# An mLSTM layer and its expert MLP on one core: weight loads on a second queue, low weight parts on GpSimd, one run of k times v, and a new order

## The chip, the cores and the metric

The kernel runs on one core of a Trainium2 chip. A core has five engines that work side by side, each through its own queue in program order: TensorE (PE, matmuls), VectorE (DVE), ScalarE (ACT), GpSimd (POOL) and SyncE (SP), which here only issues DMAs. An instruction that has to wait for another engine holds everything behind it on its own queue. The metric is the device time of one execution in microseconds (us). The time before is 543.33 us, the median of 543.33, 537.8 and 544.72.

## The reference

Four sequences with eight heads of width 40 run through a gated recurrence of 768 steps; its output, 3072 tokens by 320, runs through an MLP with 2048 hidden channels:

```
m_new = max(f[t] + m, i[t])
C = exp(f[t]+m-m_new) * C + exp(i[t]-m_new) * v[t] k[t]^T
n = exp(f[t]+m-m_new) * n + exp(i[t]-m_new) * k[t]
y[t] = sigmoid(o[t]) * (C q[t]) / max(|n q[t]|, 1)
h = y @ w_in;  g = h * erf(softplus(h));  out = g @ w_out
```

The two weights, w_in (320 x 2048) and w_out (2048 x 320), come as float64, eight bytes a number.

## The kernel before

The recurrence is done in 6 chunks of 128 time steps. An attention step s is one chunk c of one sequence b (s = 4c + b, 24 in all). It takes exponentials of gate differences (`pe`, `ex`), masks them on GpSimd (`sel`), multiplies them with q times k (`S`, `w`), sums over v (`ph`), and carries a state per sequence (`pk`, `sk`, `sa`): k times v, weighted (`vg`), is added to the state after each chunk but the last. `den`, `yg`, `y` finish the columns of y, `tr` turns them on TensorE, and `xh`, `xl` take them out of PSUM as a high and a low part. From chunk 1 on q and k are themselves split into high and low parts (`khi`, `klo`, `qhi`, `qlo`) and stacked by DMAs from `parts` to `stk`.

Two attention steps give 256 tokens. For these the MLP runs in 4 groups of 512 hidden channels, so there are 48 groups. A group has `up` (32 matmuls, h from x and w_in, line 818), a chain of activations that alternates between ScalarE and VectorE (`hb`, `a`, `a2`, `sq`, `b`, `ah`, `ab`, `w`, `wh`, `gh`, `gl`), and `dn` (24 matmuls with w_out, lines 887, 888, 890). Every matmul operand is kept as a high part and a low part; `gh` (line 868) and `gl` (line 873) are those of the MLP's middle. The first `dn` of a group needs `gh`, the last ones `gl`.

The weights are decoded on the chip, in 26 pieces: 16 of w_out (128 x 320, named `('o', n)`) and 10 of w_in (128 x 512, `('i', part, k)` and the tails `('t', i)`, the last 64 rows of two parts). A piece is scaled on ScalarE (`val`, line 707), gets its low mantissa bits by three VectorE operations (`bits`, lines 712, 713, 715), is rounded to the high part on ScalarE (`hi`, line 720), and gives the low part through TensorE: `dif` multiplies the value with the identity and subtracts the high part in PSUM (lines 725, 726), from where ScalarE copies it (`lo`, line 730). The raw bytes are loaded by SP: w_out into tiles called `parts`, two of them, three pieces each; w_in into the ten buffers that the MLP uses later as `hb`, `n0`, `n1`, `gh`, `gl`. All loads go over SP's one queue.

The order of all instructions on all engines is written out by hand: each part has a number in a table (`ATT`, `MLP`, `DEC`, `LOAD` and others), which is added to the start of its unit, and the program emits the parts sorted by that sum. So a queue's content follows from the tables, and a part waits on its engine where the data aren't there yet.

Of the kernel before, what the change touches and what calls it, by code (L numbers as in the profile page):

```python
# [99 lines left out]
ATT_NEXT = {'load': -108.5865,  # L100
    'loadv': -65.7264,
    'khi': -43.9486,
    'qhi': -36.8481,
    'klo': 33.0974,
    'qlo': 4.1048,
    'stk0': -62.7653,
    'stk1': 33.0459,
    'rows': -112.0,
    'pe0': -92.4353,
    'pe1': -82.6231,  # L110
    'ex0': -85.3469,
    'ex1': -74.7973,
    'sel0': -83.8594,
    'sel1': -59.1013,
    'S0': -64.4044,
    'S1': -29.3249,
    'vg0': -46.0099,
    'vg1': -19.402,
    'w0': -39.4592,
    'w1': -14.1493,  # L120
    'th': -41.0893,
    'pq': -109.6295,
    'qa': -38.5364,
    'ph0': -10.0541,
    'ph1': -6.3375,
    'ph2': 5.1946,
    'ph3': 6.4602,
    'pk0': -35.9301,
    'pk1': -7.3506,
    'sa0': 27.0234,  # L130
    'sa1': -6.4202,
    'sk0': -34.6458,
    'sk1': -0.3263,
    'den': 17.2106,
    'yg': 28.411,
    'y': 30.5578,
    'tr': 34.3008,
    'xh': 35.0968,
    'xl': 36.9102}
ATT = {'load': -38.0873,  # L140
    'loadv': -22.0289,
    'khi': -26.4131,
    'qhi': -24.304,
    'klo': -21.0673,
    'qlo': -20.9744,
    'stk0': -13.01,
    'stk1': -20.7116,
    'rows': -35.0,
    'pe0': -16.191,
    'pe1': -27.6979,  # L150
    'ex0': -14.5235,
    'ex1': -17.8549,
    'sel0': -13.8199,
    'sel1': -15.9236,
    'S0': -5.8456,
    'S1': -11.6692,
    'vg0': -8.7917,
    'vg1': -11.6286,
    'w0': -5.765,
    'w1': -10.6719,  # L160
    'th': -5.5334,
    'pq': -27.7455,
    'qa': -20.3849,
    'ph0': 1.4564,
    'ph1': 1.6614,
    'ph2': 2.8445,
    'ph3': 3.6732,
    'pk0': 6.9497,
    'pk1': -1.5624,
    'sa0': 7.8642,  # L170
    'sa1': 7.8309,
    'sk0': 10.4729,
    'sk1': 17.4327,
    'den': 7.2966,
    'yg': 10.4519,
    'y': 11.8501,
    'tr': 12.5049,
    'xh': 15.9467,
    'xl': 18.6409}
# [803 lines left out]
```

## Time and profile before

| | |
|---|---|
| Time, median of three | 543.33 us (537.8 to 544.72) |
| The profiled execution | 542.79 us, span 541.1 us |
| Mean granted TensorE clock | 0.987 |
| TensorE busy | 521.8 us (96%) |
| VectorE, ScalarE busy | 435.9 us (81%), 448.2 us (83%) |
| GpSimd busy | 92.4 us (17%) |
| Moved by DMA | 58.85 MB, of which 33.40 MB read from HBM |
| DMA queues of the program | one, q1 |

The profiled execution took 1.69 us more than its span from the first to the last instruction. Matmuls are pipelined: the length of one in a row (282 ns for a 128 x 256) is longer than the distance to the next (about 0.12 us), so costs on TensorE are read from the starts of successive rows. Shares of busy time are a mean over stages; the program has a start of about 48 us in which weights and first inputs arrive, a stretch up to about 150 us in which decoding, attention and MLP overlap, a regular part up to about 520 us, and an end.

### The profile page before, as it was taken

Reading aid. Unit: us, or ns where it says so; the run is one execution under the profiler, and the core shown is the slowest. Engines: PE = TensorE matmul, PEld = TensorE weight load, DVE = VectorE, ACT = ScalarE, POOL = GpSimd, SP = SyncE. Lnnn points to the kernel's source line nnn. Section 1 sums busy time; section 2 is a strip of 40 time slices with the busy share of each in tenths; the row PEclk is TensorE's granted clock in tenths of the full one; section 3 lists DMA queues with packets and bytes.
Section 4 is the critical chain, followed back from the end, with each engine's and each line's share of the span. In section 5 each row is a group of like instructions: output and inputs, shape, how many; then the busy total and the mean of one; then the engine's idle time right before and its main releaser. Section 6 shows DMA issues by size and latency. Waiting matters only on the chain.

```text
span 541.1 us, 10846 instructions
## 1 busy us (share of the span) xinstructions
PE 521.8 (96%) x4086; PEld 491.9 (91%) x4086; DVE 435.9 (81%) x693; ACT 448.2 (83%) x714; POOL 92.4 (17%) x112
## 2 busy tenths in 40 slices
PE   3989999999899999999999999999999999999997
PEld 2757799899899999999999999999999999999986
DVE  5987899979788878888888898788898678776663
ACT  5776999989868978979878978878979889889993
POOL 3220001312211211211211211211211220200000
PEclk9996999999899999999999999999999999999999
DMA  8996114504504503404513504513504514400000
GB/s 272 276 324 214 40 34 134 153 27 144 150 2 152 165 25 124 150 16 152 155 35 116 157 17 138 166 38 106 167 8 135 162 44 137 140 1 26 0 25 24
DMA packets 28302, 58.85 MB, mean 109 GB/s; under 512 B 4156, under 2 KB 8764, under 8 KB 28252
## 3 DMA queue, kind: packets, MB, share of 16 engines
q1 hardware_dynamic: 28252, 58.18, 34.8%
q8 instruction: 32, 0.52, 0.4%
q14 instruction: 18, 0.15, 0.1%
HBM read 33.40 MB, written 3.93 MB: 69 GB/s over the span
## 4 chain that ended last, share of the span: by engine, by line
PE 84%; DMA 6%; DVE 4%; ACT 3%; issue 1%; SPq 1%; POOL 0%; DVEq 0%; ACTq 0%; POOLq 0%
PE h L818 32%; PE po L887 10%; PE po L890 10%; PE po L888 9%; PE pa L629 7%; DMA n<-in_w_in_dram 4%; PE pa L626 4%; PE pa L586 3%; PE pa L639 3%; PE pa L725 2%; DMA stk<-parts 2%; PE pa L566 2%; PE pa L678 1%; PE pa L589 1%; SPq L554 1%
## 5 line engine op out<-in xcount | busy, mean ns | idle before, releaser
L818 PE MATMUL h<-xh,wh 128*128 128x256 f32 x576 | 160.1, 287 | 0.0
L818 PE MATMUL h<-xl,wh 128*128 128x256 f32 x576 | 157.3, 282 | 0.0
L887 PE MATMUL po<-woh,gh 128*128 128x320 f32 x384 | 122.4, 330 | 2.1 <-ACT o_sb L896 1.3
L888 PE MATMUL po<-wol,gh 128*128 128x320 f32 x384 | 114.9, 310 | 0.0
L818 PEld LDWEIGHTS h<-xh,wh 128*128 128x128 f32 x576 | 109.6, 190 | 1.9 <-issue 1.0
L818 PEld LDWEIGHTS h<-xl,wh 128*128 128x128 f32 x576 | 109.5, 190 | 0.2
L818 PE MATMUL h<-xh,wl 128*128 128x256 f32 x384 | 108.3, 282 | 0.0
L873 DVE TENSOR_TENSOR gl<-hb,gh 128x1024 fp32r<-128x1024 f32 x48 | 59.7, 1243 | 21.8 <-ACT gh L868 16.6
L577 POOL TENSOR_SCALAR_AFFINE_SELECT dm<-dm 128x512 f32<-128x512 f32 x48 | 47.2, 985 | 170.2 <-ACT dm L573 162.2
L887 PEld LDWEIGHTS po<-woh,gh 128*128 128x128 f32 x384 | 72.8, 190 | 2.7 <-ACT o_sb L896 1.6
L868 ACT ACTIVATE gh<-hb 128x1024 fp32r<-128x1024 f32 x48 | 50.9, 1060 | 28.3 <-DVE hb L863 27.8
L888 PEld LDWEIGHTS po<-wol,gh 128*128 128x128 f32 x384 | 72.9, 190 | 0.6
L818 PEld LDWEIGHTS h<-xh,wl 128*128 128x128 f32 x384 | 73.0, 190 | 0.0
L890 PE MATMUL po<-woh,gl 128*128 128x320 f32 x384 | 72.6, 319 | 0.0
L855 DVE SCALAR_TENSOR_TENSOR n<-n,n 128x1024 f32<-128x1024 f32 x48 | 58.7, 1224 | 14.9 <-ACT n L847 12.2
L851 DVE SCALAR_TENSOR_TENSOR n<-n,hb 128x1024 f32<-128x1024 f32 x48 | 61.8, 1288 | 4.3 <-ACT n L842 4.2
L863 DVE SCALAR_TENSOR_TENSOR hb<-n,hb 128x1024 f32<-128x1024 f32 x48 | 58.4, 1217 | 7.6 <-ACT n L859 7.4
L828 ACT ACTIVATE hb<-h 128x512 f32<-128x512 f32 x96 | 57.3, 597 | 6.1 <-PE h L818 3.3
L859 ACT ACTIVATE n<-n 128x1024 f32<-128x1024 f32 x48 | 51.4, 1070 | 11.4 <-DVE n L855 11.3
L890 PEld LDWEIGHTS po<-woh,gl 128*128 128x128 f32 x384 | 58.9, 188 | 1.1
L834 ACT ACTIVATE n<-h 128x512 f32<-128x512 f32 x96 | 57.8, 602 | 0.0
L629 PE MATMUL pa<-kvo,dm 128*128 128x41 f32 x384 | 54.8, 273 | 0.0
(102 smaller groups left out, 896.4 us busy)
## 6 DMA issues: line engine op xcount, KB each, us to landing
stk<-parts SPq DMA_DIRECT2D x120, 160.0 KB
kvo<-in_kvo_dram SPq DMA_DIRECT2D x24, 484.0 KB
parts<-in_w_out_dram SPq DMA_DIRECT2D x5, 960.0 KB
parts<-in_qk_dram SPq DMA_DIRECT2D x20, 208.0 KB
q_t<-in_qk_dram SPq DMA_DIRECT2D x20, 208.0 KB
out_dram<-o_sb SPq DMA_DIRECT2D x24, 160.0 KB
stk<-in_qk_dram SPq DMA_DIRECT2D x4, 416.0 KB
hb<-in_w_in_dram SPq DMA_DIRECT2D x2, 512.0 KB
```

Source lines behind the costliest of these rows:

```text
L629: nc.tensor.matmul(v.ph[:, 2 * p + j], v.w[j][:, p], v.v1[:, 2 * p + j], start=(c == 0), stop=(c == 0 or j == 1))
L818: nc.tensor.matmul(v.h[n // 2][:, n % 2 * T:(n % 2 + 1) * T], w, m, start=(q == 0), stop=(q == len(ops) - 1))
L828: nc.scalar.activation(v.hb[:, hs], v.h[i], AF.Copy)
L834: nc.scalar.activation(v.a[:, hs], v.h[i], AF.Tanh, scale=PARAMS[0], bias=PARAMS[1])
L851: nc.vector.scalar_tensor_tensor(out=v.a, in0=v.a, scalar=PARAMS[8], in1=v.hb, op0=ALU.add, op1=ALU.mult)
L855: nc.vector.scalar_tensor_tensor(out=v.a, in0=v.a, scalar=PARAMS[9], in1=v.b, op0=ALU.mult, op1=ALU.add)
L859: nc.scalar.activation(v.a, v.a, AF.Tanh, scale=PARAMS[10], bias=PARAMS[11])
L863: nc.vector.scalar_tensor_tensor(out=v.hb, in0=v.a, scalar=1.0, in1=v.hb, op0=ALU.add, op1=ALU.mult)
L873: nc.vector.tensor_tensor(v.gl, v.hb, v.gh.bitcast(F32), op=ALU.subtract)
L887: nc.tensor.matmul(po[k, b], v.gh[:, ts], woh[:, w], start=(j == 0), stop=False)
L888: nc.tensor.matmul(po[k, b], v.gh[:, ts], wol[:, w], start=False, stop=False)
L890: nc.tensor.matmul(po[k, b], v.gl[:, ts], woh[:, w], start=False, stop=(j == NFF - 1))
```

## The change

Five edits. (1) The ten loads of w_in (lines 748 and 763, twelve DMAs) are issued by ScalarE. (2) `dif` is gone with its two matmuls per piece and its PSUM tile, as is the negated identity; `lo` is now a subtraction on GpSimd, value less high part, both in SBUF. (3) `pk0` and `pk1`, two runs of four matmuls in two PSUM tiles, become one part `pk` of eight that alternates between the two halves of one tile. (4) The copy of y's last 64 columns goes from GpSimd to VectorE. (5) All tables of the order have new numbers.

```
-        nc.scalar.activation(nident, ident, AF.Copy, scale=-1.0)
...
+            @at('pk')
+            def _():
+                v.pk = psum(NPR, V1)
+                for p in range(NPR):
+                    for j in range(2):
+                        nc.tensor.matmul(v.pk[64 * j:64 * j + D, p], v.kn[:, 2 * p + j], v.vg[j][:, p], start=True, stop=True)
...
-            @at(f'pk{j}')
-            def _(j=j, js=js):
-                v.pk[j] = pk = psum(NPR, V1)
-                for p in range(NPR):
-                    nc.tensor.matmul(pk[js, p], v.kn[:, 2 * p + j], v.vg[j][:, p], start=True, stop=True)
...
-            nc.gpsimd.tensor_copy(y[:, 320:384], y[:, 256:320])
+            nc.vector.tensor_copy(y[:, 320:384], y[:, 256:320])
...
-        @at('dif')
-        def _():
-            v.z = ps_a.tile([128, 512], F32, name="pa")[:, 0:n]
-            nc.tensor.matmul(v.z, ident, v.val, start=True, stop=False)
-            nc.tensor.matmul(v.z, nident, hi(), start=False, stop=True)
-
         @at('lo')
         def _():
-            nc.scalar.activation(lo(), v.z, AF.Copy)
+            nc.gpsimd.tensor_tensor(lo(), v.val, hi().bitcast(F32), op=ALU.subtract)
...
-            nc.sync.dma_start(v.raw, w_in.bitcast(I32)[k * 128:(k + 1) * 128, part * 1024:(part + 1) * 1024])
+            nc.scalar.dma_start(v.raw, w_in.bitcast(I32)[k * 128:(k + 1) * 128, part * 1024:(part + 1) * 1024])
...
-                nc.sync.dma_start(v.raw[64 * j:64 * j + 64], w_in.bitcast(I32)[256:320, part * 1024:(part + 1) * 1024])
+                nc.scalar.dma_start(v.raw[64 * j:64 * j + 64], w_in.bitcast(I32)[256:320, part * 1024:(part + 1) * 1024])
...
-LOAD = {(0, 0): -100.853,
-    (0, 1): -70.8649,
+LOAD = {(0, 0): -633.6701,
+    (0, 1): -675.1264,
```

SP's queue before, from its first DMA on. `hb`, `gh`, `n_258`, `n_276` and `gl` receive w_in, `parts` w_out, `kvo` and `stk` are the inputs of an attention step, `gt` the gates.

```order
L429 DMA gt<-in_gates_dram 128x2x128
L405 DMA cst<-in_consts_dram 128x12
L788 DMA parts<-in_w_out_dram 128x3x640 x2
L525 DMA kvo<-in_kvo_dram 128x968 x2
L519 DMA stk<-in_qk_dram 104x1024 x2
L748 DMA hb<-in_w_in_dram 128x1024
L748 DMA gh<-in_w_in_dram 128x1024
L788 DMA parts<-in_w_out_dram 128x3x640
L763 DMA n_258<-in_w_in_dram 64x1024 x2
```

SP's queue of the changed kernel, at the same place.

```order
L430 DMA gt<-in_gates_dram 128x2x128
L407 DMA cst<-in_consts_dram 128x12
L786 DMA parts<-in_w_out_dram 128x3x640 x2
L526 DMA kvo<-in_kvo_dram 128x968 x2
L520 DMA stk<-in_qk_dram 104x1024 x2
L786 DMA parts<-in_w_out_dram 128x3x640 x2
L520 DMA stk<-in_qk_dram 104x1024
L430 DMA gt<-in_gates_dram 128x2x128
```

ScalarE's queue of the changed kernel, from its first instruction on.

```order
L761 DMA n_96<-in_w_in_dram 64x1024 x2
L746 DMA n_114<-in_w_in_dram 128x1024
L417 ACT_TABLE_LOAD
L417 ACTIVATE rhsE_77<-cst 128x1024
L746 DMA gh<-in_w_in_dram 128x1024
L746 DMA hb<-in_w_in_dram 128x1024
L464 ACTIVATE spl<-x_119 128x256 x2
L746 DMA gl<-in_w_in_dram 128x1024
L746 DMA n_143<-in_w_in_dram 128x1024
L746 DMA gl<-in_w_in_dram 128x1024
L711 ACTIVATE bits<-parts 128x320 x2
L761 DMA n_211<-in_w_in_dram 64x1024 x2
```

Before, two loads of w_in stood behind the inputs of the first two attention steps and eight further back; now seven stand on ScalarE's queue ahead of its first piece of decoding, two of them ahead of everything else. On SP the same loads as before stand ahead of `stk`, and the third load of w_out follows it directly.

VectorE's queue around the first two products of attention (`dm<-pa,dm`), in the kernel before; `bits` are pieces of decoding, from w_out (`parts`) or w_in (`hb`).

```order
L595 TENSOR_TENSOR vg<-kvo,dm 128x164 x2
L712 TENSOR_SCALAR bits<-bits 128x320
L713 SCALAR_TENSOR_TENSOR bits<-parts,bits 128x320
L715 SCALAR_TENSOR_TENSOR bits<-parts,bits 128x320
L712 TENSOR_SCALAR bits<-bits 128x320
L713 SCALAR_TENSOR_TENSOR bits<-parts,bits 128x320
L715 SCALAR_TENSOR_TENSOR bits<-parts,bits 128x320
L600 TENSOR_TENSOR dm<-pa,dm 128x512
```

The same place in the changed kernel, with four rows behind the first product.

```order
L596 TENSOR_TENSOR vg<-kvo,dm 128x164 x2
L716 TENSOR_SCALAR bits<-bits 128x320
L717 SCALAR_TENSOR_TENSOR bits<-parts,bits 128x320
L719 SCALAR_TENSOR_TENSOR bits<-parts,bits 128x320
L601 TENSOR_TENSOR dm<-pa,dm 128x512
L716 TENSOR_SCALAR bits<-bits 128x512
L717 SCALAR_TENSOR_TENSOR bits<-hb,bits 128x512
L719 SCALAR_TENSOR_TENSOR bits<-hb,bits 128x512
L596 TENSOR_TENSOR vg<-kvo,dm 128x164
```

The first product is now behind five pieces of decoding, not six, and a piece of w_in follows it at once. One piece of the second load of w_out and two more products later come two pieces of its third load, on VectorE and, with their `val`, on ScalarE.

TensorE's queue in the regular part, where k times v stands in the kernel before (`pa<-vg,kvo`); `po` are the MLP's outputs, `stk` is q times k.

```order
L586 MATMUL pa<-stk 128x128 x4
L890 MATMUL po_3012<-woh,gl 128x320 x2
L639 MATMUL pa<-vg,kvo 40x41 x4
L890 MATMUL po_3012<-woh,gl 128x320 x2
L890 MATMUL po_3051<-woh,gl 128x320 x4
```

The same in the changed kernel.

```order
L587 MATMUL pa<-stk 128x128 x4
L640 MATMUL pa<-vg,kvo 40x41 x8
L888 MATMUL po_2931<-woh,gl 128x320 x4
L627 MATMUL pa<-state_84,q_t 128x82
L630 MATMUL pa<-kvo,dm 128x41 x2
```

The forty runs of four, two per step that hands on a state, become nineteen stretches, eighteen of eight and one of sixteen; a run that stood between two matmuls of the MLP is joined to the other half of its step.

More of the change, by code (lines that the diff above doesn't have):

```diff
@@ L100 @@
[L100 to L179, printed above, removed]
@@ new lines @@
+ATT_NEXT = {'load': -156.6534,
+    'loadv': -60.4274,
+    'khi': -106.5954,
+    'qhi': -211.6908,
+    'klo': 179.8945,
+    'qlo': -14.3309,
+    'stk0': -401.7728,
+    'stk1': 105.1859,
+    'rows': -296.7179,
+    'pe0': -103.7926,
+    'pe1': -78.7968,
+    'ex0': -97.4069,
+    'ex1': -55.6452,
+    'sel0': -77.8633,
+    'sel1': -49.6155,
+    'S0': -55.5881,
+    'S1': -40.4793,
+    'vg0': -47.4185,
+    'vg1': -35.7269,
+    'w0': -43.5687,
+    'w1': -16.6082,
+    'th': -41.8574,
+    'pq': -359.4575,
+    'qa': 117.6845,
+    'ph0': -14.5258,
+    'ph1': -2.6974,
+    'ph2': -1.3244,
+    'ph3': -11.1149,
+    'pk': -25.6239,
+    'sa0': 300.4603,
+    'sa1': -158.213,
+    'sk0': 10.5361,
+    'sk1': -24.6199,
+    'den': 0.5645,
+    'yg': 25.717,
+    'y': 27.8062,
+    'tr': 29.5129,
+    'xh': 31.3893,
+    'xl': 38.2853}
@@ new lines @@
+ATT = {'load': -40.8874,
+    'loadv': -37.1974,
+    'khi': -30.7803,
+    'qhi': -34.9486,
+    'klo': -24.3981,
+    'qlo': -23.992,
+    'stk0': -16.0487,
+    'stk1': -20.9237,
+    'rows': -49.361,
+    'pe0': -15.6061,
+    'pe1': -35.2528,
+    'ex0': -11.4489,
+    'ex1': -24.7875,
+    'sel0': -10.496,
+    'sel1': -11.9304,
+    'S0': -9.5901,
+    'S1': -13.7849,
+    'vg0': -7.288,
+    'vg1': -11.599,
+    'w0': -3.5874,
+    'w1': -9.4351,
+    'th': -15.1335,
+    'pq': -34.1679,
+    'qa': -17.1663,
+    'ph0': -2.2401,
+    'ph1': 1.3585,
+    'ph2': 1.65,
+    'ph3': -1.8142,
+    'pk': -3.1091,
+    'sa0': 9.6376,
+    'sa1': 10.4814,
+    'sk0': 20.4876,
+    'sk1': 13.6725,
+    'den': 8.6591,
+    'yg': 7.2627,
+    'y': 8.6594,
+    'tr': 10.545,
+    'xh': 17.4758,
+    'xl': 20.0822}
@@ new lines @@
+DEC = {'val': 3.5278,
+    'bits': 10.4958,
+    'hi': 13.2128,
+    'lo': 13.8278}
+MLP_FIRST = {'up0': -18.5334,
+    'up1': -15.7894,
+    'up2': -14.7159,
+    'up3': -10.7645,
+    'hb0': -7.363,
+    'a0': -5.886,
+    'hb1': 5.7283,
+    'a1': -3.7905,
+    'a2': 8.0021,
+    'sq': 16.3615,
+    'b': 17.0411,
+    'ah': 21.51,
+    'ab': 26.2409,
+    'w': 29.1197,
+    'wh': 35.8626,
+    'gh': 39.0148,
+    'gl': 45.9697,
+    'dn0': 45.2167,
+    'dn1': 49.2466,
+    'dn2': 49.4193,
+    'dn3': 50.334,
+    'dn4': 40.5578,
+    'dn5': 41.6552,
+    'dn6': 52.6278,
+    'dn7': 57.1304,
+    'o0': 333.337,
+    'o1': 27.8299}
@@ new lines @@
+MLP = {'up0': 9.9187,
+    'up1': 10.4113,
+    'up2': 14.1245,
+    'up3': 14.5284,
+    'hb0': 20.0323,
+    'a0': 19.8669,
+    'hb1': 23.5849,
+    'a1': 21.3006,
+    'a2': 25.5555,
+    'sq': 27.4935,
+    'b': 29.4977,
+    'ah': 29.494,
+    'ab': 29.8728,
+    'w': 35.3778,
+    'wh': 35.6791,
+    'gh': 39.4692,
+    'gl': 42.5606,
+    'dn0': 56.0931,
+    'dn1': 56.1967,
+    'dn2': 57.853,
+    'dn3': 58.0956,
+    'dn4': 59.2514,
+    'dn5': 59.5093,
+    'dn6': 60.6131,
+    'dn7': 61.9819,
+    'o0': 65.1678,
+    'o1': 74.131}
```

365 lines of the change are left out of this document (156 added, 209 removed).

## The prediction

> **What bounds the kernel now.** I read the busy times first, then the busy times by stretch, then the order of time around the first groups of the MLP. The busy line of the page and the stretches (busy us of PE, weight loads, VectorE, ScalarE, GpSimd; clock; DMA share; GB/s):
>
> ```profile
> PE 521.8 (96%) x4086; PEld 491.9 (91%) x4086; DVE 435.9 (81%) x693; ACT 448.2 (83%) x714; POOL 92.4 (17%) x112
> ...
> 0.00:10.00 10.00, 1.31 (x7) 0.76 (x8) 5.00 (x15) 4.37 (x8) 3.79 (x18) 1.00 0.73 255
> 10.00:48.00 38.00, 35.78 (x198) 23.60 (x197) 31.09 (x66) 28.12 (x63) 7.74 (x12) 0.91 1.00 298
> 48.00:60.00 12.00, 12.00 (x76) 9.66 (x75) 8.43 (x19) 9.44 (x20) 0.00 (x0) 0.86 0.23 80
> 60.00:90.00 30.00, 30.00 (x222) 27.65 (x221) 28.21 (x52) 29.01 (x55) 2.61 (x4) 1.00 0.19 54
> 90.00:110.00 20.00, 18.80 (x156) 18.06 (x155) 19.10 (x31) 18.89 (x30) 4.36 (x4) 1.00 0.51 157
> 110.00:150.00 40.00, 38.18 (x307) 36.60 (x305) 33.71 (x54) 33.31 (x53) 9.45 (x8) 0.96 0.36 108
> 150.00:520.00 370.00, 370.00 (x3029) 360.70 (x3028) 299.87 (x456) 313.75 (x477) 64.49 (x66) 1.00 0.30 93
> ```
>
> By the total the kernel is TensorE's. By stretch three things follow each other. Up to 48 us the DMA engines are full (share 1.00, 298 GB/s). From 60 to 110 us TensorE, VectorE and ScalarE are all full: 48.8, 47.3 and 47.9 of 50 us. From 150 to 520 us TensorE never rests, VectorE is busy 81% and ScalarE 85% of the time. So in the second of these stretches less work for TensorE alone brings nothing. Which engine is ahead there shows in the order of time, at the MLP's first and third group (start, length):
>
> ```profile
> 71.09 1.05 ACT L868 ACTIVATE gh<-hb 128x1024 fp32r<-128x1024 f32 x1
> 73.44 1.22 DVE L873 TENSOR_TENSOR gl<-hb,gh 128x1024 fp32r<-128x1024 f32 x1
> 74.29 0.39 PE L887 MATMUL po<-woh,gh 128*128 128x320 f32 x1
> ...
> 92.81 1.06 ACT L868 ACTIVATE gh<-hb 128x1024 fp32r<-128x1024 f32 x1
> 93.90 1.23 DVE L873 TENSOR_TENSOR gl<-hb,gh 128x1024 fp32r<-128x1024 f32 x1 [0.46 <-ACT gh L868]
> 94.73 0.50 PE L887 MATMUL po<-woh,gh 128*128 128x320 f32 x1
> ```
>
> The third group's first down matmul starts 0.9 us after its gh is there (92.81 + 1.06 = 93.87), and its gl ends at 95.13, just ahead of need. Up to here TensorE runs at the heels of ScalarE and VectorE; behind it TensorE has work enough to the end. So the time after the change is the new date of the third gl plus TensorE's work behind it. VectorE's idle time ahead of that date is 5.00 + 6.91 + 3.57 + 1.79 = 17.3 us up to 90 us, with 0.5 us more to 95 us: 17.8 us.
>
> **What the change takes from TensorE.** The subtraction of a piece, 128 x 320 between MLP matmuls and 128 x 512 ahead of another matmul:
>
> ```profile
> 51.53 0.70 PE L725 MATMUL pa<-bits,ident 128*128 128x320 f32 x2
> 51.83 0.55 PE L726 MATMUL pa<-woh,nident 128*128 128x320 f32 x1
> 52.22 0.28 PE L818 MATMUL h<-xh,wh 128*128 128x256 f32 x1
> ...
> 30.25 1.11 PE L725 MATMUL pa<-bits,ident 128*128 128x512 f32 x2
> 30.90 0.69 PE L726 MATMUL pa<-stk,nident 128*128 128x512 f32 x1
> 31.43 0.39 PE L566 MATMUL pa<-rhsE,splB 128*128 128x512 bf16 x1
> ```
>
> From start to the next start: 0.69 us and 1.18 us, so 16 x 0.69 + 10 x 1.18 = 22.8 us in all. All of it lies ahead of the third gl, where TensorE doesn't set the date, so I count it at nothing; if TensorE did set it, it would be worth up to 22.8 us (a rival, below). For k times v:
>
> ```profile
> 236.62 0.28 PE L818 MATMUL h<-xh,wh 128*128 128x256 f32 x1
> 236.74 0.28 PE L818 MATMUL h<-xl,wh 128*128 128x256 f32 x1
> 236.95 0.50 PE L639 MATMUL pa<-vg,kvo 128*40 128x41 f32 x8
> 237.38 0.39 PE L818 MATMUL h<-xh,wh 128*128 128x256 f32 x1
> 237.61 0.28 PE L818 MATMUL h<-xl,wh 128*128 128x256 f32 x1
> ```
>
> Neighbours start 0.12 us apart; into the run it is 0.21, behind it 0.23. Changing to and fro costs 0.09 + 0.11 = 0.20 us a run. One run a step in place of two saves that once for each of 20 steps; 16 of them (chunks 1 to 4) lie behind the third gl, in TensorE's own stretch: -3.2 us. Whether the alternation between the two halves changes the 0.43 us of a run isn't shown; its bounds are nothing and half of two runs, 16 x 0.43 = -6.9 us. I take nothing, the cost as the row has it.
>
> **What it moves in the start.** The loads, their sizes, and when three things ran:
>
> ```profile
> kvo<-in_kvo_dram SPq DMA_DIRECT2D x24, 484.0 KB
> parts<-in_w_out_dram SPq DMA_DIRECT2D x5, 960.0 KB
> stk<-in_qk_dram SPq DMA_DIRECT2D x4, 416.0 KB
> hb<-in_w_in_dram SPq DMA_DIRECT2D x2, 512.0 KB
> gt<-in_gates_dram SPq DMA_DIRECT2D x6, 128.0 KB
> ...
> 15.36 0.38 SPq L788 DMA_DIRECT2D parts<-in_w_out_dram  x1
> ...
> 19.07 0.68 DVE L600 TENSOR_TENSOR dm<-pa,dm 128x512 f32<-128x512 f32 x1
> ...
> 23.01 0.49 ACT L707 ACTIVATE bits<-parts 128x320 f32<-128x320 f32 x1 [1.71 <-DMA parts<-in_w_out_dram]
> ```
>
> First a test on before. 255 GB/s for 10 us is 2490 KB (of 1024 bytes), 298 GB/s is 291 KB a us. The third load of w_out has gates and constants (134), two parts (1920), two kvo (968), two stk (832) and two of w_in (1024) ahead, with itself 5838 KB: 10 + 3348/291 = 21.5 us. It was waited for until 23.0, so I add 1.5 us.
>
> Now SP's queue has 3438 KB up to the first stk and 4814 KB up to the third load of w_out, and ScalarE's queue up to 5120 KB of w_in beside it. The program of before has one queue (q1), so how two share isn't shown; the bounds are SP's first and ScalarE's first, and between them I take equal parts, since each engine's share is full with either. Then the first stk is there when 6876 KB have moved, at 25.1 + 1.5 = 26.6 us, and the third load of w_out at 9628 KB, at 34.5 + 1.5 = 36.0 us. By the Trainium skill ("DMA: Bandwidth & Descriptors", section on queues, rings and completion order) each DMA engine goes round the queues that have work, a packet at a time, and both queues use the same sixteen. By that rule it would be nearly this equal division; no run here shows it yet.
>
> The first product of attention waits for that stk. On VectorE stand behind it a w_in piece that needs nothing of attention, and everything else. Ahead of it are the gates (about 3.7 of the 5.00 us in the first 10), five pieces of 1.3 us and two small products, 10.9 us in all. At 27 us VectorE has then been idle 16.1 us (before, the product ran at 19.07). Behind it 5.9 us of work, to 32.9; then the third load's pieces, first ScalarE's scaling (0.5 us), at 36.5: 3.6 us more. On ScalarE the two scalings of that load hold the tanh of the o gate, two high parts, the scaling of a w_in tail and an exponential of the third step. The piece's durations:
>
> ```profile
> L712 DVE TENSOR_SCALAR bits<-bits 128x320 int32<-128x320 int32 x16 | 5.6, 351 | 2.4 <-ACT bits L707 2.4
> L713 DVE SCALAR_TENSOR_TENSOR bits<-parts,bits x16: 491/493/802, 8.9 to 85.6; 128x320 int32<-128x320 int32 x16
> L577 POOL TENSOR_SCALAR_AFFINE_SELECT dm<-dm x48: 636/1032/1501, 10.5 to 470.3; 128x512 f32<-128x512 f32 x48
> L851 DVE SCALAR_TENSOR_TENSOR n<-n,hb 128x1024 f32<-128x1024 f32 x48 | 61.8, 1288 | 4.3 <-ACT n L842 4.2
> L730 ACT ACTIVATE wol<-pa 128x320 fp32r<-128x320 f32 x16 | 7.0, 437 | 0.0
> L730 ACT ACTIVATE wl<-pa 128x512 fp32r<-128x512 f32 x8 | 4.7, 582 | 1.1 <-PE pa L726 1.1
> PE pa L586 <- DMA stk<-parts: 3.0, 2, 1.8
> ```
>
> So 19.7 us idle by 36.5 us. From there I put 2 us to the third gl (before: 1.79 in 30 us from 60 on; ScalarE is relieved of 16 x 0.437 + 10 x 0.582 = 12.8 us of copies, which feeds VectorE sooner). Together 21.7 in place of 17.8: **+3.9 us**, from about 0 (SP first: the stk comes at 14.8, but w_in's first piece behind it only at 26.5) to +6 (ScalarE first). ScalarE's twelve issues, at about 0.4 us as SP's 0.38, lie mostly in its first 10 us, of which it used 4.37.
>
> VectorE's other work ahead of the third gl is the same 26 pieces and the same parts of attention, and in addition one ah (1.29 us) and four copies of y's columns, put at 0.17 each (half of L712's 0.35 at a fifth of its width): **+2.0 us**. The remaining copies fall where VectorE has 19% left.
>
> GpSimd now subtracts 26 times, 19 of them behind the last long wait. The trace shows such neighbours holding each other: line 577 takes 0.64 us alone and up to 1.50, and line 713 0.49 or, when it collides, 0.80, that is 0.31 more. I take 0.2 us of VectorE for each, since not each collides: **+3.8 us**, from 1 (one in six) to 12 (each holds VectorE for 0.64). Only the skill has the subtraction itself: by "GPSIMD Engine Reference" (section 3.1), 2.6 cycles an element, an estimate of 0.7 and 1.1 us.
>
> Behind the third gl, TensorE's waits for the stack copies (3.0 us) should shrink, as the copies stand earlier on SP: -1, from 0 to -3.
>
> **The sum.** 541.1 + 3.9 + 2.0 + 3.8 - 3.2 - 1.0 = 546.6 us span; the profiled execution took 1.69 more than its span (542.79), so **548 us**, 1% above the profiled execution and above the median of 543.33.
>
> **The rivals.**
> - *The loads don't hold each other*, or VectorE's idle time comes out as before: the first term is 0, 544 us. For it: all bytes of the start are the same, and before also waited for data. Against: seven loads of w_in that are used late now stand beside those used first.
> - *GpSimd holds VectorE* (the slower end). Its subtraction reads two operands where line 577 reads one, and each of 19 costs VectorE 0.9 us, within 577's own 0.64 to 1.50: 17 in place of 3.8, 561 us. It decides above 0.5 us each (554 us). For it: 577 more than doubles under VectorE's long operations. Against: line 713's usual duration is its shortest. The skill's "SBUF — State Buffer" (who interferes with whom) has it that a VectorE operation with two SBUF inputs and a GpSimd one that reads SBUF exclude each other for the whole instruction; by that rule the price is near this end, while 713's 0.31 us agrees only with part of it.
> - *TensorE sets the date after all*: ScalarE's 12.8 us and the 22.8 us of matmuls both let the start close up, VectorE's idle time of 17.8 us nearly goes, and all 22.8 + 4.0 us show: 516 us, with half of it 530. For it: TensorE was full from 48 to 90 us. Against: VectorE 94% busy beside it, with more work now, and data that arrive no earlier.
>
> **Chances.** Forecast 0.47, loads 0.21, GpSimd 0.20, TensorE 0.12. A difference under 2% (about 11 us: below 532, above 554) can't be told from none. Faster: TensorE's 0.12, and 0.03 of the first two with the alternation's 6.9 us: 0.15. Slower: 0.17 of GpSimd's 0.20 and 0.05 of the forecast: 0.22. Same: 0.63. The range for 8 in 10 leaves out most of TensorE's case and the upper half of GpSimd's: 534 to 561.
>
> **What would show it.** The first product on VectorE near 27 us in place of 19.07, and ScalarE's first scaling of the third load of w_out waiting for its DMA to about 36; the third gl's end near 105 in place of 95.13; VectorE's lines 717 and 719 (713 and 715 before) longer beside subtractions on GpSimd; TensorE idle ahead of 100 us but full from 150 on, with the k times v runs at one entry and exit a step. A third gl before 90 us would make the forecast wrong, as would a regular part whose four groups no longer take what they took.

## The result and the profile after

The changed kernel takes 565.8 us (median of 4, 565.6 to 569.7) against 541.8 us (median of 4) for the kernel before on the same chip: 1.048 times as long, with a 95% interval of 1.043 to 1.053. The forecast was 548 us with a range of 534 to 561. The profiled execution has a span of 564.1 us, 23.0 more than before, and 17.5 more than the sum of 546.6.

The page of the changed kernel, busy times:

```profile
PE 504.3 (89%) x4008; PEld 484.4 (86%) x4008; DVE 462.7 (82%) x717; ACT 438.0 (78%) x687; POOL 99.2 (18%) x114
```

TensorE is busy 17.5 us less than before and rests 60 us in place of 19. The stretches show where (columns as in the prediction: busy us of PE, weight loads, VectorE, ScalarE, GpSimd; clock; DMA share; GB/s):

```profile
0.00:10.00 10.00, 0.00 (x0) 0.00 (x0) 3.02 (x10) 3.06 (x4) 3.00 (x16) 1.00 0.80 225
10.00:48.00 38.00, 21.00 (x128) 17.63 (x128) 27.72 (x50) 17.67 (x37) 16.85 (x20) 0.61 0.89 275
...
60.00:90.00 30.00, 24.38 (x185) 23.26 (x184) 29.26 (x46) 23.00 (x42) 11.45 (x9) 0.83 0.12 34
90.00:110.00 20.00, 16.64 (x118) 15.66 (x117) 19.56 (x32) 16.90 (x29) 7.49 (x7) 0.91 0.34 108
...
150.00:520.00 370.00, 357.56 (x2950) 347.85 (x2950) 310.01 (x482) 303.57 (x466) 49.62 (x51) 0.99 0.31 96
520.00:570.00 50.00, 39.64 (x293) 39.04 (x291) 25.25 (x21) 33.23 (x45) 0.00 (x0) 0.99 0.04 14
```

Up to 48 us VectorE is busy 30.7 us, before 36.1; from 60 to 110 us it alone is full (48.8 of 50), where before three engines were. And from 150 to 520 us TensorE, which never rested there, now rests 12.4 us.

The order of time: VectorE's first piece of w_out, TensorE's product for the first attention step, and on VectorE the first product of attention and the third gl (lines 600 and 873 before):

```profile
17.53 0.33 DVE L716 TENSOR_SCALAR bits<-bits 128x320 int32<-128x320 int32 x1 [6.95 <-ACT bits L711]
22.42 3.06 PE L590 MATMUL pa<-stk 40*128 40x128 f32 x16 [7.66 <-ACT dm L574]
28.70 0.68 DVE L601 TENSOR_TENSOR dm<-pa,dm 128x512 f32<-128x512 f32 x1
...
111.86 1.21 DVE L871 TENSOR_TENSOR gl<-hb,gh 128x1024 fp32r<-128x1024 f32 x1
```

The first product stands at 28.7 us (19.07 before, forecast 27), but it did not wait for its `stk`: that load landed at 22.3 us, its matmuls were over by 25.5, and VectorE came to the product 3 us later, without a wait just ahead of it. What VectorE had waited for is the first piece of w_out, 6.95 us. The third gl ends at 113.1 us (95.1 before, forecast 105). So of the 23.0 us, 18.0 arise ahead of the third gl and 5.0 behind it; the sum had 9.7 and -4.2. These two numbers, the end of the third gl and the rest of the span behind it, are what the experiments are read by.

In the start, ScalarE and then SyncE issue and wait as follows (the number ahead of the arrow is the idle time before the instruction; ACTq and SPq are DMA issues):

```profile
10.91 0.33 ACTq L746 DMA_DIRECT2D gl<-in_w_in_dram  x1
16.14 0.34 ACTq L746 DMA_DIRECT2D n<-in_w_in_dram  x1
16.52 0.44 ACTq L746 DMA_DIRECT2D gl<-in_w_in_dram  x1
17.01 0.87 ACT L711 ACTIVATE bits<-parts 128x320 f32<-128x320 f32 x2 [7.39 <-DMA parts<-in_w_out_dram]
```

```profile
5.42 2.02 SPq L526 DMA_DIRECT2D kvo<-in_kvo_dram  x2
...
25.87 0.40 SPq L786 DMA_DIRECT2D parts<-in_w_out_dram  x1
```

The first scaling of w_out starts at 17.0 us, although its load had landed at 10.89: it stands behind two issues at 16.14 and 16.52 on its own engine. The semaphores in the trace show what these waited for. In this program all loads take turns on eight semaphores, whichever engine issues them, and an issue waits until the load that used its semaphore before has landed. The issue at 10.91 has that of w_out's first load (landed 10.89), the issue at 16.14 that of the second (landed 16.12). The third load of w_out, issued at 15.36 before, is issued at 25.87, when VectorE has read the last piece out of its buffer (25.80).

What became of VectorE's two bit operations on 128x320 (the group rows of VectorE up to the third gl, before and after, and then of the fifth experiment, which has GpSimd's subtraction alone):

```profile
L715 DVE SCALAR_TENSOR_TENSOR bits<-parts,bits 128x320 int32<-128x320 int32 x16 | 8.6, 540 | 0.5
L713 DVE SCALAR_TENSOR_TENSOR bits<-parts,bits 128x320 int32<-128x320 int32 x16 | 8.3, 519 | 0.5
```

```profile
L719 DVE SCALAR_TENSOR_TENSOR bits<-parts,bits 128x320 int32<-128x320 int32 x16 | 11.2, 697 | 0.5
L717 DVE SCALAR_TENSOR_TENSOR bits<-parts,bits 128x320 int32<-128x320 int32 x16 | 8.6, 536 | 0.5
```

```profile
L715 DVE SCALAR_TENSOR_TENSOR bits<-parts,bits 128x320 int32<-128x320 int32 x16 | 12.0, 749 | 0.5
```

The second of the two now takes 0.70 us in the mean in place of 0.54. To have this for all operations I add up, for each VectorE operation up to the third gl, its duration less the shortest of the same line and form in these runs, and call the sum the lengthening: 3.6 us before, 19.6 us after.

### The profile page after: what moved, and what is told of

Its sections match the earlier page's. It is cut to its first block, busy times and chain, and to the rows that moved or that the text cites. A ratio compares the mean times of both kernels' runs of the same rounds, so it can differ in the third digit from the quotient of the medians.

```text
span 564.1 us, 10569 instructions
## 1 busy us (share of the span) xinstructions
PE 504.3 (89%) x4008; PEld 484.4 (86%) x4008; DVE 462.7 (82%) x717; ACT 438.0 (78%) x687; POOL 99.2 (18%) x114
## 4 chain that ended last, share of the span: by engine, by line
PE 41%; DVE 21%; ACT 17%; DMA 12%; issue 5%; SPq 3%; POOL 1%; ACTq 0%; DVEq 0%; POOLq 0%
PE h L816 16%; PE pa L630 5%; PE po L888 5%; PE po L885 5%; DMA stk<-parts 5%; PE po L886 4%; DMA kvo<-in_kvo_dram 4%; DVE bits L717 3%; DVE bits L719 2%; SPq L555 2%; PE pa L627 2%; ACT n L840 2%; ACT gh L866 2%; PE pa L587 2%; DVE bits L716 2%
## 5 line engine op out<-in xcount | busy, mean ns | idle before, releaser
L816 PE MATMUL h<-xh,wh 128*128 128x256 f32 x576 | 167.5, 299 | 0.0
L816 PE MATMUL h<-xl,wh 128*128 128x256 f32 x576 | 160.9, 287 | 0.0
L885 PE MATMUL po<-woh,gh 128*128 128x320 f32 x384 | 117.3, 317 | 6.5 <-ACT gh L866 4.6
L816 PEld LDWEIGHTS h<-xh,wh 128*128 128x128 f32 x576 | 112.9, 196 | 0.5 <-issue 0.4
L816 PEld LDWEIGHTS h<-xl,wh 128*128 128x128 f32 x576 | 112.7, 196 | 0.3
L816 PE MATMUL h<-xh,wl 128*128 128x256 f32 x384 | 110.4, 287 | 0.0
L888 PE MATMUL po<-woh,gl 128*128 128x320 f32 x384 | 80.4, 322 | 0.8 <-DVE gl L871 0.8
L861 DVE SCALAR_TENSOR_TENSOR hb<-n,hb 128x1024 f32<-128x1024 f32 x48 | 59.4, 1237 | 22.7 <-ACT n L857 22.7
L816 PEld LDWEIGHTS h<-xh,wl 128*128 128x128 f32 x384 | 75.1, 196 | 0.0
L849 DVE SCALAR_TENSOR_TENSOR n<-n,hb 128x1024 f32<-128x1024 f32 x48 | 59.9, 1248 | 5.0 <-ACT n L840 4.7
L866 ACT ACTIVATE gh<-hb 128x1024 fp32r<-128x1024 f32 x48 | 51.1, 1065 | 16.1 <-DVE hb L861 11.6
L630 PE MATMUL pa<-kvo,dm 128*128 128x41 f32 x384 | 58.0, 286 | 2.4 <-DVE dm L601 2.3
```

The lines of the kernel that those rows point to most:

```text
L630: nc.tensor.matmul(v.ph[:, 2 * p + j], v.w[j][:, p], v.v1[:, 2 * p + j], start=(c == 0), stop=(c == 0 or j == 1))
L816: nc.tensor.matmul(v.h[n // 2][:, n % 2 * T:(n % 2 + 1) * T], w, m, start=(q == 0), stop=(q == len(ops) - 1))
L849: nc.vector.scalar_tensor_tensor(out=v.a, in0=v.a, scalar=PARAMS[8], in1=v.hb, op0=ALU.add, op1=ALU.mult)
L861: nc.vector.scalar_tensor_tensor(out=v.hb, in0=v.a, scalar=1.0, in1=v.hb, op0=ALU.add, op1=ALU.mult)
L866: nc.scalar.activation(v.gh, v.hb, AF.Copy)
L885: nc.tensor.matmul(po[k, b], v.gh[:, ts], woh[:, w], start=(j == 0), stop=False)
```

## The experiments

The table has the profiled execution of each run: end of the third gl, VectorE's busy and idle time up to there (from the timeline and from one stretch up to that end), the span behind it; then the median of the timed runs and the ratio to the kernel before on the same chip. The kernel before takes 539.6 to 541.8 us (medians) on the chips of these runs, and a profiled execution lies up to 2.7 us off its row's median, so differences between rows of some 2 us show nothing.

| Run | third gl | busy | idle | behind | median us | ratio [95%] |
|---|---|---|---|---|---|---|
| before | 95.1 | 77.1 | 18.0 | 446.0 | 541.8 | 1 |
| after | 113.1 | 94.3 | 18.8 | 451.0 | 565.8 | 1.048 [1.043, 1.053] |
| e1 low parts set to zero | 104.2 | 79.1 | 25.1 | 455.0 | 559.7 | 1.034 [1.028, 1.039] |
| e2 loads on SyncE | 115.3 | 95.4 | 19.9 | 453.6 | 568.0 | 1.052 [1.048, 1.055] |
| e3 low parts on VectorE | 117.6 | 91.4 | 26.3 | 453.6 | 572.8 | 1.060 [1.057, 1.063] |
| e4 regular tables of before | 116.7 | 94.0 | 22.7 | 446.4 | 563.8 | 1.043 [1.040, 1.046] |
| e5 before + low parts on GpSimd | 106.4 | 92.1 | 14.4 | 443.0 | 552.5 | 1.020 [1.015, 1.025] |
| e6 before + loads on ScalarE | 106.2 | 77.1 | 29.1 | 445.6 | 553.3 | 1.021 [1.015, 1.026] |
| e7 before + one run | 96.3 | 77.0 | 19.3 | 434.6 | 531.1 | 0.980 [0.974, 0.985] |
| e8 four edits, old order | 112.2 | 93.3 | 18.8 | 435.3 | 551.2 | 1.018 [1.012, 1.023] |
| e9 one run, halves one by one | 95.1 | 77.1 | 17.9 | 439.6 | 537.0 | 0.995 [0.991, 1.000] |
| e10 before + low parts as a copy | 91.8 | 79.2 | 12.6 | 447.3 | 539.2 | 0.998 [0.996, 1.001] |
| e11 after, loads as before | 107.3 | 95.7 | 11.7 | 451.8 | 562.4 | 1.041 [1.037, 1.044] |
| e12 e8 with the new regular part | 117.6 | 94.2 | 23.4 | 450.5 | 568.5 | 1.051 [1.047, 1.055] |
| e13 after, low halves earlier | 115.8 | 94.5 | 21.3 | 436.4 | 554.2 | 1.025 [1.019, 1.030] |
| e14 e7 + y's columns by VectorE | 96.2 | 77.4 | 18.8 | 434.4 | 531.1 | 0.983 [0.977, 0.989] |

Where only the start was edited, the span behind the third gl stays within 4 us of its partner's (e5, e6 and e10 of before; e1, e2, e3 and e11 of after). TensorE's granted clock up to the third gl, 0.76 in the changed kernel and 0.95 before, doesn't set its date: with the same order e2 and e13 have 0.96 there and a third gl no earlier.

### Each edit alone, in the old order

The edit of e5, and that of e6 (likewise at line 763):

```
-        @at('dif')
...
-            nc.scalar.activation(lo(), v.z, AF.Copy)
+            nc.gpsimd.tensor_tensor(lo(), v.val, hi().bitcast(F32), op=ALU.subtract)
```

> The kernel before with one edit: low weight parts by a subtraction on GpSimd (no matmuls, no copies by ScalarE for them); order and queues as before. G: VectorE's rows in the first 100 us get some 10 to 14 us longer, the third gl ends near 102 to 107 us in place of 95, time 542 -> 548 to 554. If TensorE or ScalarE set the date of the third gl (22.8 us and 12.8 us are taken from them): 530 to 538.

```
-            nc.sync.dma_start(v.raw, w_in.bitcast(I32)[k * 128:(k + 1) * 128, part * 1024:(part + 1) * 1024])
+            nc.scalar.dma_start(v.raw, w_in.bitcast(I32)[k * 128:(k + 1) * 128, part * 1024:(part + 1) * 1024])
```

> The kernel before with one edit: w_in's loads issued by ScalarE at the same places of the order. Q: the loads come earlier than before relative to SP's, ScalarE is held at its issues, the start is longer, 545 to 550. G and O: 541 to 543.

The edit of e7 is the changed kernel's `pk`, and e8 has all four edits; in the old tables pk takes the place of pk1 (in the first two steps an earlier one, with sk0 and sk1 behind it):

```
-    'pk0': 6.9497,
-    'pk1': -1.5624,
+    'pk': -1.5624,
...
                 for p in range(NPR):
-                    nc.tensor.matmul(pk[js, p], v.kn[:, 2 * p + j], v.vg[j][:, p], start=True, stop=True)
+                    for j in range(2):
+                        nc.tensor.matmul(v.pk[64 * j:64 * j + D, p], v.kn[:, 2 * p + j], v.vg[j][:, p], start=True, stop=True)
```

> The kernel before with one edit: k times v in one run of eight (in the first four steps the part and its state copies had to move by some places). By the forecast's term: 16 to 20 times 0.20 us less on TensorE in its own stretch, -3 to -4 us, 538 to 539. If the alternation of the two halves also shortens a run by half: -10 us, 532. If the run's place in the regular part costs a wait: 541 or more.

> All edits of the change with the order of before (k times v in one run as in the run on that edit alone, no dif parts). G: slower than before by what the subtraction alone brings, less 3 us for the runs: 545 to 552. O (the new order is what costs): 536 to 541. Q: loads on ScalarE's queue at their old places cost 3 to 8 us on top of the others.

e14 adds to e7:

```
-            nc.gpsimd.tensor_copy(y[:, 320:384], y[:, 256:320])
+            nc.vector.tensor_copy(y[:, 320:384], y[:, 256:320])
```

> The kernel before with k times v in one run (531.1 us) and y's columns copied by VectorE in place of GpSimd. GpSimd's copy takes 0.70 us and VectorE is busy 81% of the time. Theory A: 4 copies of 0.17 us ahead of the third gl show, the others fall into idle time: 531 to 533. Theory B: the transposes of y wait for GpSimd's copy, and a faster one brings them forward: 527 to 530.

**Low parts on GpSimd (e5): +10.7 us** (552.5 against 541.8), all of it ahead of the third gl (+11.3; behind it the profiled execution is 3.0 us shorter). VectorE's lengthening rises from 3.6 to 18.9 us, 15.3 for 26 subtractions, or 0.59 us each; 3.6 us of it come back as less idle time. VectorE's and then GpSimd's operations of e5 in the same microseconds:

```profile
24.71 1.23 DVE L715 SCALAR_TENSOR_TENSOR bits<-hb,bits 128x512 int32<-128x512 int32 x1
...
27.06 1.07 DVE L712 TENSOR_SCALAR bits<-bits 128x320 int32<-128x320 int32 x1
```

```profile
24.11 1.28 POOL L724 TENSOR_TENSOR wol<-bits,woh 128x320 fp32r<-128x320 f32 x1 [1.32 <-ACT woh L720]
26.68 1.27 POOL L724 TENSOR_TENSOR wl<-bits,wh 128x512 fp32r<-128x512 f32 x1 [1.29 <-ACT wh L720]
```

The shift that takes 0.35 us alone takes 1.07, and ends 0.2 us behind the subtraction: it seems to have been held until then. Over all of e5, the 49 VectorE operations that lie beside a subtraction have 17.0 of the 18.9 us.

**Loads on ScalarE's queue (e6): +11.5 us**, again all ahead of the third gl (+11.1), and here it is idle time of VectorE (29.1 in place of 18.0). ScalarE's DMA issues and the scaling behind them, and what VectorE then waits for:

```profile
15.32 0.44 ACTq L748 DMA_DIRECT2D hb<-in_w_in_dram  x1
...
28.74 0.34 ACTq L748 DMA_DIRECT2D hb<-in_w_in_dram  x1
32.00 0.33 ACTq L748 DMA_DIRECT2D gl<-in_w_in_dram  x1
32.43 0.48 ACT L707 ACTIVATE bits<-parts 128x320 f32<-128x320 f32 x1 [6.80 <-DMA stk<-in_qk_dram]
```

```profile
32.95 0.33 DVE L712 TENSOR_SCALAR bits<-bits 128x320 int32<-128x320 int32 x1 [7.99 <-ACT bits L707]
```

SyncE issued the first of these at 5.39; on ScalarE it stands behind that engine's own scalings and exponentials and goes out 10 us later. And it works the other way too: from 25.6 to 32.4 us ScalarE does nothing but two more issues, at 28.74 and 32.00, and the scaling for which VectorE waits 8 us follows right behind the second. The row names a DMA as what it waited for; it is the one for which the issue just ahead was held. The issue at 28.74 has the semaphore of SyncE's third load of w_out (landed 28.72), the one at 32.00 that of a `stk` (landed 31.98). SyncE issued the same three loads within 1.1 us (18.28 to 19.39), and where it stood and waited, no computation stood behind it.

**k times v in one run (e7): -10.7 us**, all behind the third gl (434.6 in place of 446.0). **y's columns (e14): nothing**, 531.1 with and without. **All four in the old order (e8): +9.4 us**; the single prices add up to 10.7 + 11.5 - 10.7 + 0 = 11.5. The changed kernel takes 14.6 us more than that. The third gl differs by only 0.9 us (112.2 and 113.1): the new order's cost lies behind it, 451.0 in place of 435.3.

### Why one run gains so much

e9 has the run of e7, with the loops exchanged:

```
-                for p in range(NPR):
-                    for j in range(2):
+                for j in range(2):
+                    for p in range(NPR):
```

> The kernel before with k times v in one run of sixteen, as in the run that took 531.1 us, but with the eight products of the first half of the columns ahead of the eight of the second, in place of taking the halves in turn. Theory A: halves in turn overlap (there a run of sixteen takes 0.44 us from its first start to the next line's start, a run of eight before took 0.43); then this run takes about 0.85 us and the kernel 531 + 16 x 0.41 = about 538 us. Theory B: the gain is that of leaving out one entry and exit of the run, whatever the order within; then 531 us as before.

A step's run in e7, and in e9 (start, length; x16 counts two records for each matmul, as x8 did before):

```profile
232.03 0.28 PE L818 MATMUL h<-xl,wh 128*128 128x256 f32 x1
232.25 0.51 PE L636 MATMUL pa<-vg,kvo 128*40 128x41 f32 x16
232.68 0.39 PE L818 MATMUL h<-xh,wh 128*128 128x256 f32 x1
```

```profile
234.21 0.69 PE L636 MATMUL pa<-vg,kvo 128*40 128x41 f32 x16
234.83 0.39 PE L818 MATMUL h<-xh,wh 128*128 128x256 f32 x1
```

In turn, both halves together take 0.43 us (0.44 at most in all 15 such runs behind 115 us), no more than one half took before. One after the other they take 0.62. So a step saves 2 x 0.43 + 0.20 - 0.43 = 0.63 us in e7, 16 x 0.63 = 10.1 us, and e7 measured 10.7. In e9 it should be 16 x 0.44 = 7.0; its profiled span is 6.4 us below that of before, but by the ratio on one chip it is only 2.7 us faster (interval 0 to 5). Where the rest went is open. e9's time is near that of theory A, but theory A's 0.85 us for its run was too much: a second half that follows costs 0.19 and not 0.42.

### What the low parts cost in the changed kernel

e1 writes zeros (the low weight parts are left out), e3 has VectorE subtract:

```
-            nc.gpsimd.tensor_tensor(lo(), v.val, hi().bitcast(F32), op=ALU.subtract)
+            nc.gpsimd.memset(lo().bitcast(F32), 0.0)
```

> The changed kernel, but GpSimd fills the low weight parts with zeros in place of the subtraction (the low parts of the weights are left out); every wait and the order stay. Theory G (GpSimd's reads of SBUF lengthen VectorE's two-operand operations: VectorE's decoding rows are some 14 us longer in the first 100 us than their shortest): this lengthening mostly goes, the third gl ends near 100 us in place of 113, time 566 -> about 553. Theory Q (loads on ScalarE's queue delay the start) and theory O (the regular part's new order waits more): nothing of theirs is touched, about 564 to 566, with the saving of GpSimd's own time at most 2 us.

```
-            nc.gpsimd.tensor_tensor(lo(), v.val, hi().bitcast(F32), op=ALU.subtract)
+            nc.vector.tensor_tensor(lo(), v.val, hi().bitcast(F32), op=ALU.subtract)
```

> The changed kernel with the 26 subtractions on VectorE. They are 16 x 0.49 + 10 x 0.69 = 14.7 us of new work there. G: they replace about as much lengthening by GpSimd, so third gl and time stay within 4 us of the changed kernel (562 to 568). Q and O without G: VectorE is full in the start, so the work adds: 575 to 581.

In e1 the lengthening falls from 19.6 to 4.3 us, and VectorE's busy time by 15.2; but its idle time rises by 6.3, since now it waits for data again. What remains is 8.9 us at the third gl and 6.1 us in time. The zeros wait for no high part, so they are written earlier than the subtractions ran; still they lie beside VectorE's operations for 11 us in all. On VectorE itself (e3) the lengthening is 3.3 us but the work 14 us more, and it is slower still by 7 us: GpSimd was not the worst place.

e10 tells whether it matters what GpSimd does in that time:

```
-            nc.gpsimd.tensor_tensor(lo(), v.val, hi().bitcast(F32), op=ALU.subtract)
+            nc.gpsimd.tensor_copy(lo(), v.val)
```

> The kernel before with the low parts by GpSimd, but as a copy of the value, one operand read in place of two (the subtraction of the high part is left out, so the low parts hold the whole weights). With the subtraction VectorE's operations up to the third gl were 15.3 us longer in sum than in the kernel before, and the kernel took 552.5 us. Theory A: GpSimd holds VectorE whenever it reads or writes the shared memory, for as long as it runs; then a copy costs by its duration (the copy of 128x64 on GpSimd took 0.70 us and that of 32x256 0.74 to 1.10), lengthening stays over 8 us and the time is 547 to 552. Theory B: it is the second operand that GpSimd reads; then the lengthening falls to about 4 us, and the time to 541 to 543.

A copy of 128x320 takes 0.59 us in the mean where the subtraction takes 1.04, the lengthening is 6.2 us, and the time is that of before (539.2 against 540.4). Theory A's 547 to 552 did not come, but theory B isn't shown either: the copy is shorter as well, and does not wait for the high part. That one operand is enough to hold VectorE shows elsewhere, below. Besides, e10 has no dif matmuls and no ScalarE copies of low parts: 22.8 us of TensorE and 12.8 of ScalarE removed, and with VectorE hardly touched they bring 1.2 us, with an interval from nothing to 2.2. The third gl does come earlier, by 3.3 us in the profiled execution, but most of that doesn't reach the end.

### The loads in the new order

e2 issues the loads of w_in by SyncE at the changed kernel's places; e11 does so at the places of before, with the whole table LOAD of before:

```
-            nc.scalar.dma_start(v.raw, w_in.bitcast(I32)[k * 128:(k + 1) * 128, part * 1024:(part + 1) * 1024])
+            nc.sync.dma_start(v.raw, w_in.bitcast(I32)[k * 128:(k + 1) * 128, part * 1024:(part + 1) * 1024])
```

> The changed kernel with the twelve loads of w_in issued by SP again, at the same places of the order (so ahead of kvo and stk on one queue). Q by ScalarE being held at its issues: the gates come at 3.5 us in place of 5.9, the first scaling of w_out at about 14 us in place of 17.0, the time is 3 to 5 us shorter, 561 to 563. Q by the bytes in front alone, G and O: the first product stays near 28 us and the time near 566.

```
-LOAD = {(0, 0): -633.6701,
+LOAD = {(0, 0): -100.853,
...
```

> The changed kernel, with all loads of w_in and w_out issued by SyncE at the places that the table of before gives them. All else as changed. Theory A: the early loads of w_in stand in front of those that are used first, and that costs the start; then the first scaling of w_out is back at about 8 us from 17.0, the first product at 19 to 22 in place of 28.7, VectorE's idle time up to the third gl falls from 12.4 to 5 to 8 us, and the time from 565.8 to 558 to 561. Theory B: VectorE is full from 30 us on and only the collisions with GpSimd set the third gl, so earlier data bring nothing: 563 to 567.

In e2 nothing is won (568.0): ScalarE is no longer held, but on one queue four loads of w_in go out ahead of w_out's first, which lands at 16.2 us in place of 10.9, so its scaling starts at 16.2 all the same. e2 trades one delay for the other and can't price either. With the old places (e11), which take both away, the first scaling is back at 7.2 us, the first product at 19.7, VectorE's idle time at 11.7 us, and the third gl 5.8 us earlier. In time this gives 3.4 us by the medians (565.8 to 562.4), between the ranges of the two theories: theory A by its dates, with less behind them than it had.

### Behind the third gl

e4 has the changed kernel's start with the regular tables of before; e12 the reverse, the old start with the new regular tables:

```
-ATT = {'load': -40.8874,
+ATT = {'load': -38.0873,
...
```

> The changed kernel with the order of the regular part taken from before (tables ATT, MLP, MLP_END and the three spacings; its two pk runs stay one). O: four groups take 40.9 us again in place of 41 to 44, TensorE's idle time of 12.4 us between 150 and 520 us mostly goes, the time is 6 to 10 us shorter, 556 to 560. G and Q: the loss lies in the start, the time stays at 564 to 567.

> All four edits with the order of before, as in the run that took 551.2 us, but with the changed kernel's tables for the regular steps and MLP groups (ATT, MLP, MLP_END and the three spacings). Theory A: the regular part of the new order costs some 5 us a chunk, as TensorE waits there for the stack copies of k and q (7.7 us from 150 to 520 us) and for vg (4.0 us), and 3.3 chunks make 15 us; then 563 to 567, with such waits in the trace. Theory B: the regular order is as good as the old, and the 15 us come from where the start goes over into it; then 550 to 555.

e12 settles the place: 568.5, 17.3 us above e8, and behind the third gl 450.5 as after, not 435.3 (its third gl is 5.4 us later than e8's as well). e4 gains only 2 us; behind its third gl it takes 446.4. From the first low half of k of chunk 2 to that of chunk 3 it takes 79.2 us, as e8 does (78.9; 85.8 in the changed kernel), but from chunk 1 to chunk 2 it takes 86.6 where e8 takes 76.6. So it loses where the new start and the old regular part meet; why, no run shows.

TensorE's waits from 120 to 520 us, in e8 and in the changed kernel (us in total, times, longest):

```profile
PE pa L581 <- DMA stk<-parts: 2.4, 2, 1.8
PE pa L581 <- ACT n L826: 0.2, 1, 0.2
```

```profile
PE pa L587 <- DMA stk<-parts: 7.7, 6, 2.1
PE pa L587 <- DVE vg L596: 4.0, 3, 1.8
PE po L885 <- ACT o_sb L894: 1.9, 2, 1.3
```

One such wait in the changed kernel, followed back: TensorE's product of q and k, the low halves of k and q of the same step on VectorE, and the train of copies on SyncE (six of this step, then six of the next):

```profile
240.26 0.78 PE L587 MATMUL pa<-stk 120*128 120x128 f32 x4 [1.92 <-DMA stk<-parts]
```

```profile
231.32 1.12 DVE L540 TENSOR_TENSOR parts<-parts 104x512 fp32r<-104x512 f32 x1
232.37 0.68 DVE L548 TENSOR_TENSOR parts<-q_t,parts 104x512 fp32r<-104x512 f32 x1
```

```profile
228.13 15.89 SPq L555 DMA_DIRECT2D stk<-parts  x12
```

The first copy goes out at 228.1, the second, with k's low half, only at 232.5, as line 540 ends (232.44); the high half was there since 226.3, from ScalarE, and SyncE stood at this copy from 229.0 on. The sixth copy, for which the product waits, lands at 240.1. e13 moves the low halves alone:

```
-    'klo': -24.3981,
-    'qlo': -23.992,
+    'klo': -28.5,
+    'qlo': -28.4,
```

> The changed kernel with one edit in its table: the low halves of k and q in the regular steps (lines 540 and 548) 4.1 and 4.4 us earlier, which puts those of a chunk's second step some six VectorE operations earlier (ahead of gl and of the next group's products). Theory A: they make the stack copies late, and TensorE waits for these 7.7 us from 150 to 520 us; then this wait falls to 3 us or less and the time from 565.8 to 558 to 562. Theory B: the copies are late for another reason (SyncE's queue, in which twelve of them stand in one train of 16 us), or the gl that is now behind costs as much; then 564 to 568.

VectorE's low halves of the same step, TensorE's same product, and TensorE's waits from 120 to 520 us in e13:

```profile
228.39 0.69 DVE L540 TENSOR_TENSOR parts<-parts 104x512 fp32r<-104x512 f32 x1
228.99 0.69 DVE L548 TENSOR_TENSOR parts<-q_t,parts 104x512 fp32r<-104x512 f32 x1
```

```profile
238.83 0.56 PE L587 MATMUL pa<-stk 120*128 120x128 f32 x4
```

```profile
PE pa L567 <- DVE xl L695: 2.5, 5, 0.7
PE po L885 <- ACT o_sb L894: 1.9, 2, 1.6
PE pa L682 <- DVE kvo L673: 0.6, 1, 0.6
```

The low halves stand 2.9 us earlier here (5.6 in the next step), the second copy goes out at 229.4, the waits for the copies and for vg are gone, and the kernel takes 554.2 us, 11.6 less, more than the 4 to 8 of theory A. Behind the third gl it takes 436.4, as e8 does: the whole loss of the new order there hung on the place of these operations. It is more than the waits listed: behind the third gl TensorE is idle 19.9 us in the changed kernel and 9.7 in e8 and in e13, and its granted clock is 0.992 in place of 1.000 and 0.999, an estimate of 3 us of its 431 busy ones. The new order with the low parts on TensorE, as before, was not tried. The fastest of all is e7 (and e14), 531.1 us.

## Why the prediction was wrong

The frame held to some 4 us: the time is the end of the third gl plus what TensorE has behind it. Of the terms:

1. **GpSimd's hold, +3.8: mis-sized, the largest miss ahead of the third gl.** "I take 0.2 us of VectorE for each, since not each collides": it is 15.3/26 = 0.59 us for each of all 26, in the changed kernel 16.0 us of lengthening. The rival had the mechanism right; its sum (0.9 for each of 19 is 17 us) came near with a price too high for too few. "Line 713's usual duration is its shortest" was no evidence against it: up to the third gl GpSimd was busy 14.1 us before and 43.7 in the changed kernel. By the Trainium skill ("SBUF — State Buffer", who interferes with whom) a VectorE operation with two SBUF inputs contends with a GpSimd one that reads SBUF, not with one that only writes: e1's writes leave the lengthening at 4.3 us, which agrees. That sentence doesn't cover the shift of line 712, which has one input and was held too (1.07 us).
2. **The loads, +3.9: mis-sized, and the dates that came near did so by luck.** With GpSimd's hold absent VectorE's idle time is 25.1 us (e1) in place of 18.0, and with the old places it falls by the same 7.1 us (18.8 to 11.7, e11). That is above the bound of 6. The first product came at 28.7 (forecast 27), with 16.4 us of idle time ahead of it (forecast 16.1), but not by the forecast's path. That had two queues share full DMA engines and the product wait for its `stk` to 26.6. The DMA engines were busy only 0.80 (to 10 us) and 0.89 (to 48 us) of the time, `stk` landed at 22.3, and VectorE's long wait was for the first piece of w_out, since an issue of w_in stood ahead of ScalarE's scaling and waited itself. "ScalarE's twelve issues, at about 0.4 us" counted their length and not that wait. The third load of w_out landed at 34.84 (forecast 36), late because its buffer came free late; ScalarE scaled it at 34.92 without having waited for it, and up to 36.5 us VectorE was idle 16.6 us (forecast 19.7). In the changed kernel the idle time is nearly that of before (18.8), since a VectorE that is held has less of it: the two terms together are 18, not 7 + 16. I had added them as independent.
3. **VectorE's other work, +2.0:** 94.3 - 77.1 - 16.0 = 1.2 us.
4. **dif matmuls and ScalarE's copies at nothing:** right in time (1.2 us or nothing, e10), though the third gl comes 3.3 us earlier without them. The rival that TensorE sets the date falls.
5. **k times v, -3.2: mis-sized.** "I take nothing" for the alternation: entry and exit are 0.20 us as worked out, but the halves in turn save 0.43 more; -10.1 by the rows, -10.7 measured. The far bound that the prediction named (-3.2 and -6.9) is where it came out.
6. **The stack-copy waits, -1.0: wrong in sign, and the step that failed behind the third gl.** "As the copies stand earlier on SP": they wait for k's low half, which the new order puts too late on VectorE. The regular part was costed by SyncE's order and not by the engine that feeds it. It cost 15.7 us (435.3 to 451.0 in the profiled executions, some 14 by the medians), of which e13 takes 14.6 back by moving two lines.

In sum: ahead of the third gl 18.0 in place of 9.7; behind it -10.7 + 15.7 = +5.0 in place of -4.2; 8.3 + 9.2 is the 17.5 us missed. The chance of 0.22 for slower held mostly GpSimd's case, which by itself was worth +10.7 us; that the loss behind the third gl would come on top was in no rival.

## What to carry to other kernels

Before a part goes to GpSimd, look at what VectorE runs in the same microseconds: a cost per collision seen while GpSimd is nearly idle says nothing of one where each operation meets another. A load that is issued from a computing engine's queue stands in that queue, and so does what it waits for: look at which semaphore the issue waits for, and at what stands behind it. When an order is written anew, follow each transfer back to the instruction that makes its data, on that engine's list; a queue on which the copy stands early proves nothing. And try edits one at a time: here one of the five was worth 2%, and the rest took it away threefold.

## What was not expected of the hardware

- Eight matmuls with 40 columns of weights, four for each half of the columns, take 0.43 us in turn, 0.62 us half by half, and two separate runs of four 0.86 us and an entry and exit more. In turn the second of a pair starts 0.007 us behind the first.
- GpSimd's select (line 578), which reads one operand, holds VectorE too. Line 540 of the changed kernel takes 0.68 us where it meets none for more than 0.05 us, and 1.10 to 1.12 in twelve of its 20 executions, all of which overlap one by 0.56 us or more; before, none overlapped and all took 0.68:

```profile
L540 DVE TENSOR_TENSOR parts<-parts x20: 679/1118/1124, 107.1 to 487.0; 104x512 fp32r<-104x512 f32 x20
```

```profile
L539 DVE TENSOR_TENSOR parts<-parts x20: 681/682/685, 90.0 to 464.9; 104x512 fp32r<-104x512 f32 x20
```

So an order decides collisions too: in e13, with the low halves elsewhere, none of the 20 meets a select, and one meets a subtraction and a copy (1.25 us).
